# Re-planning the first tile of a fused attention and MLP kernel, and splitting its last store

## Chip, cores and metric

The kernel runs on one core of a Trainium2 chip. The metric is the device time of one execution in microseconds (us). A profile of one execution of the kernel before is at hand: its span (first to last instruction) and the start and length of every instruction on the engines PE (TensorE; PEld is its weight load), DVE (VectorE), ACT (ScalarE), POOL (GpSimd) and SP (the engine that issues most DMAs). Times below are microseconds from the span's start.

## The reference

Attention over 4 batches, 8 heads, 768 positions and head size 64, followed by a two-layer MLP. Some heads ("retrieval") use the full causal mask; the others keep only a few first positions ("sinks") and a window.

```python
scores = scale * np.matmul(q, k.transpose(0, 1, 3, 2))
causal = rel >= 0                      # rel = query position - key position
stream_keep = causal & (is_sink | ((rel >= 0) & (rel < window)))   # 4 sinks, window 64
mask = np.where(retr, causal, stream_keep)                          # per head
a = softmax(np.where(mask, scores, -1e9))
x = matmul(a, v)  ->  [3072 tokens, 512]
h = x @ w_in                           # [3072, 2048]
out = (h - np.tanh(h)) @ w_out         # [3072, 512]
```

## The kernel before

The 3072 tokens are cut into 12 tiles of 256; three tiles make one batch. A tile t is worked in four head pairs; n = 4t + pair numbers the pairs. The stages of a pair:

- `load` (L236): q, k and v of the tile come in as fp32 through SP's queue; the first two tiles in halves of four heads.
- `cast_qk`, `cast_v` (L410 to L449): copies to fp16. v gets a 65th column of ones (scaled), so that the row sum comes out of the same matmul. `scale_v` (L451) makes `vf`, v times a flag per head, for key blocks that lie wholly outside the window: flag 1 for retrieval heads, 0 for the others; there are four such blocks a batch.
- `st_T` (L478): TensorE transposes q and k of the pair into one PSUM tile `tp`; copies take q to `qT` and the two heads of k to `kz`, a buffer of [128, 2, 768] in which each head's rows stand beside zeros. `zero_kz` (L346) writes these zeros once, for two batches' buffers (kz0, kz1).
- `st_S` (L530): scores into a PSUM tile `sc`, exponential on ScalarE into `pt`, and on VectorE a multiplication by the 0/1 mask `m4` (L379), which is built from the select tiles `A4`, `sinks` and the retrieval flags (`retr_i`, `nz`, `rflag`, `thr`).
- `st_A` (L586): `av` = pt times v (and vf); then `rinv` and `x` on VectorE divide by the row sum.
- `st_X` (L628): x is transposed into `xT`, the input of the MLP.

The MLP has `H_unit` (L653: eight matmuls of 256 columns into PSUM `ph`, tanh `th` on ScalarE, `gt` = h - tanh(h) on VectorE; eight units a tile) and `O_mms` (L690: per block of 128 tokens, 16 matmuls of 512 columns into `po`, an eviction on ScalarE to `ot`, a store by SP).

[...] two tiles `sc` of two banks each (used by scores and by tp), one `m` (av, later xp), two `h` (ph), one `o` (po, and xp of the first tile).

The order of the work is not written out by hand. Every stage calls `op` with an engine, a cost in ns, and the keys it reads and writes; the class `Plan` plays the list through with these costs, engine by engine, and at each step emits the ready operation that was recorded first. This settles each engine's instruction order at build time. The semaphores are put in afterwards by the tile framework, from the tiles that instructions touch; they don't depend on the planner's keys. [...]

```python
        for k in r:
            if k in self.writer:
                deps.add(self.writer[k])
            self.readers.setdefault(k, []).append(i)
```

The first tile is recorded pair by pair with its transposes, scores, products; the H units of tile 0 and the attention of tile 1 are laid side by side by a table (`plan`, L784), and the output matmuls of a tile follow one tile later (`LAG`).

Of the kernel before, what the change touches and what calls it, by code (L numbers as in the profile page):

```python
# [7 lines left out]
FP32 = mybir.dt.float32  # L8
FP16 = mybir.dt.float16
I32 = mybir.dt.int32  # L10

XS = 4096.0
TT = 256
NB = TT // 128


class Plan:
# [3 lines left out]

    ENGINES = ("PE", "ACT", "DVE", "POOL", "SP")
    OVERLAP = {"PE": 0, "ACT": 100, "DVE": 88, "POOL": 60, "SP": 0}
    RESULT = {"PE": 200, "ACT": 0, "DVE": 0, "POOL": 0, "SP": 0}

    def __init__(self, bufs):
# [6 lines left out]
    def op(self, eng, ns, fn, r=(), w=(), dma=None, prio=None, port=False):  # L33
        i = len(self.ops)
        deps = set()
        for k in r:
            if k in self.writer:
                deps.add(self.writer[k])
            self.readers.setdefault(k, []).append(i)
        for k in w:  # L40
            if k in self.writer:
                deps.add(self.writer[k])
            deps.update(self.readers.get(k, ()))
            self.writer[k] = i
# [102 lines left out]
def kernel(  # L147
# [12 lines left out]
    nc = tc.nc  # L160
# [115 lines left out]
    def load_w_out(j, w_after):  # L276
# [11 lines left out]

    retr_i = const.tile([128, 2 * H], I32, name="retr_i")
    op(  # L290
        "ACT", 400,
        lambda: nc.scalar.dma_start(
            out=retr_i[:], in_=is_retrieval.bitcast(I32).partition_broadcast(128)
        ),
        w=["retr"], dma=(128, 20.0),
# [50 lines left out]
    def zero_kz(eng, s, hp, c0, c1):  # L346
        op(
            eng, (c1 - c0) * 1.06 + 20,
            lambda: engs[eng].memset(kz[s][hp][:].bitcast(FP32)[:, :, c0 // 2 : c1 // 2], 0.0),  # L349
            w=[("kz", s, hp, g) for g in range(c0 // TT, c1 // TT)],  # L350
        )

    for hp in range(HP):
        zero_kz("DVE", 0, hp, 0, S)

    nz = const.tile([128, 2 * H], FP32, name="nz")
    op(
# [93 lines left out]
    def scale_v(t):  # L451
        b, g = divmod(t, NG)
        v1, vf, lo = v1s[b], vfs[b], g * NB
        for jb in range(lo, min(lo + NB, 4)):
            fl = rflag0 if jb == 0 else rflag
            op(
                "POOL", 1053,
                lambda jb=jb, fl=fl: nc.gpsimd.tensor_mul(  # L458
                    out=vf()[:, jb, :, :], in0=v1()[:, jb, :, :],
                    in1=fl[:].unsqueeze(2).to_broadcast([128, H, D + 1]),  # L460
                ),
                r=[("v1", b, g, 0), ("v1", b, g, 1), "rflag0", "rflag"], w=[("vf", b, jb)],
            )


# [5 lines left out]
    def copy(e, dst, src):  # L471
        if e == "ACT":
            nc.scalar.copy(out=dst, in_=src)  # L473
        else:
            nc.vector.tensor_copy(out=dst, in_=src)  # L475

    def st_T(n, eq="DVE", ek=("DVE", "DVE")):
        t, hp = divmod(n, HP)  # L478
        b, g = divmod(t, NG)
        cs = slice(g * TT, (g + 1) * TT)  # L480
        tp, key = bank([128, 2, NB, 128], FP16, "sc", f"tp{n}")
        cq, ck = t16s["q", t], t16s["k", t]

        def mm():
            for x, c in enumerate((cq, ck)):
                for i in range(NB):
                    nc.tensor.transpose(  # L487
                        out=tp()[:, x, i, :], in_=c()[:, i, 2 * hp : 2 * hp + 2, :],
                        identity=ident16[:],
                    )  # L490

        op(
            "PE", 224, mm,
            r=["ident"] + [("t16" + nm, t, hp * 2 // HP) for nm in "qk"], w=[key],
        )
# [4 lines left out]
        op(  # L500
            eq, cost[eq],
            lambda: copy(eq, qT[n]()[:], tp()[:, 0, :, :].rearrange("p i c -> p (i c)")),
            r=[key], w=[(f"qT{hp}", t)],
        )
        for hh in range(2):
            p_ = slice(64 * hh, 64 * hh + 64)
            op(
                ek[hh], cost[ek[hh]],
                lambda p_=p_, hh=hh: copy(
                    ek[hh], kk[p_, hh, cs], tp()[p_, 1, :, :].rearrange("p i c -> p (i c)")  # L510
                ),
                r=[key], w=[("kz", b % 2, hp, g)],
            )


# [137 lines left out]
    def H_unit(t, u):  # L653
# [33 lines left out]
            r=[key, tk], w=[("gt", t, u)],  # L687
        )

    def O_mms(t, j0, j1):  # L690
        for j in range(j0, j1, 2):
            ts, fb = divmod(j, NFB)
            if fb == 0:
                pos[t] = bank([128, DM], FP32, "o", f"po{t}_{ts}")
            po, key = pos[t]

            def mm(fb=fb, ts=ts, po=po):
                for f in (fb, fb + 1):
                    nc.tensor.matmul(  # L699
                        out=po()[:], lhsT=gts[t]()[:, f, ts * 128 : ts * 128 + 128],  # L700
                        rhs=w_out_t[f // 4]()[:, f % 4, :],
                        start=(f == 0), stop=(f == NFB - 1),
                    )

            op("PE", 2 * 216, mm, r=[("wout", fb // 4), ("gt", t, fb // FU)], w=[key])
            if fb == NFB - 2:
                ot = lazy(o_pool, [128, DM], FP32, "ot", f"ot{t}_{ts}")
                ok = ("ot", 2 * t + ts)
                t0 = t * TT + ts * 128
                op(  # L710
                    "ACT", 597,
                    lambda ot=ot, po=po: nc.scalar.activation(  # L712
                        out=ot()[:], in_=po()[:], func=AF.Copy, scale=1.0 / XS
                    ),
                    r=[key], w=[ok],
                )
                op(
                    "SP", 420,
                    lambda ot=ot, t0=t0: nc.sync.dma_start(out=out[t0 : t0 + 128, :], in_=ot()[:]),
                    r=[ok], dma=(128, 75.0),  # L720
                )


    NU = NTT * HP
# [1 line left out]
    def scores(n):  # L726
        return [lambda gi=gi: st_S(n, gi) for gi in range(len(GROUPS[(n // HP) % NG]))]
# [17 lines left out]
            res.append(lambda: st_X(n))  # L745
        return res

    cast_qk(0, (("DVE", "DVE"), ("ACT", "DVE")), (0,))
    cast_v(0, ("POOL", "POOL"), (0,))
    cast_qk(0, (("DVE", "DVE"), ("DVE", "DVE")), (1,))  # L750
    cast_v(0, ("POOL", "POOL"), (1,))
    load(1, halves=range(2))
    for n in range(HP):
        st_T(n, "ACT", ("DVE", "ACT"))
        if n:
            for f in scores(n - 1):
                f()
        if n > 1:
            st_A(n - 2, 0)
            st_A(n - 2, 1)  # L760
        if n > 2:
            st_X(n - 3, "o")
    for f in scores(HP - 1):
        f()
    for n in (HP - 2, HP - 1):
        st_A(n, 0)
        st_A(n, 1)
        st_X(n - 1, "o")
    st_X(HP - 1, "o")
# [12 lines left out]

# [74 lines left out]
```

The softmax here doesn't subtract the row's maximum and nothing guards it: scores larger than these inputs give would overflow.

## Time and profile before

| what | us |
|---|---|
| median of three runs | 273.51 |
| lowest and highest of them | 271.87, 339.37 |
| the profiled execution | 272.34 |
| its span | 270.5 |
| PE busy in the span | 249.0 (92%) |
| DVE busy | 174.7 (65%) |
| ACT busy | 156.9 (58%) |
| POOL busy | 71.3 (26%) |

In a line of stages the columns are the window, its length, then busy time with the number of instructions for PE, PEld, DVE, ACT and POOL, the granted TensorE clock, the DMA share and GB/s. A line of the chain has start, length and what it was: engine, tile, source line. A line of the timeline has start, length (of all the merged instructions), engine, source line, operation, the tile written and the tile read, the sizes, the count, and in brackets the idle time before it and what ended that. A busy PE is not a PE at its peak, since matmuls overlap and their ends are modelled. Over the whole span the DMA engines are over 90% busy up to about 88 us, while all of q, k, v and the weights come in.

### The profile page before, as it was taken

The page shows a single profiled execution, that of the slowest core. Times are in us where ns is not written, and L with a number is a line of the kernel's source. Part 1 is how long each engine was busy: PE and PEld are TensorE (multiplying, and loading weights), DVE is VectorE, ACT ScalarE, POOL GpSimd, SP SyncE. Part 2 cuts the span into 40 slices and gives each one's busy share as a digit, 9 for nine tenths or more (in the row PEclk, how much of TensorE's full clock was granted, in tenths as well). Part 3 has the DMA queues.
Part 4 walks back from the last instruction along what each step waited for, and adds up shares of the span by engine and source line. Part 5 has one row for each costly group of instructions (what it writes and reads, how often), then busy time and mean ns, then how long its engine had stood idle before and what let it go on. Part 6 is the DMA issues. An engine that isn't in the chain of part 4 may idle for free.

```text
span 270.5 us, 6313 instructions
## 1 busy us (share of the span) xinstructions
PE 249.0 (92%) x2560; PEld 187.1 (69%) x2560; DVE 174.7 (65%) x445; ACT 156.9 (58%) x228; POOL 71.3 (26%) x130
## 2 busy tenths in 40 slices
PE   0477889999999999999999999999999999999974
PEld 0355767777778877777777777777878777776631
DVE  7587765676898765567987746567887555554410
ACT  2355645875567677564577566654657766634420
POOL 7589201364640930309603000300300000000000
PEclk9999999999999999999999999999999999999999
DMA  6999999999998982175631511010001001010101
GB/s 140 221 216 201 196 197 198 226 230 215 245 229 174 199 177 63 43 156 131 139 81 55 106 40 39 2 41 39 15 26 41 2 39 41 2 41 39 41 39 78
DMA packets 82925, 29.78 MB, mean 110 GB/s; under 512 B 75728, under 2 KB 79824, under 8 KB 82896
## 3 DMA queue, kind: packets, MB, share of 16 engines
q1 hardware_dynamic: 78528, 25.17, 43.3%
q0 software_dynamic: 4224, 4.19, 9.2%
q8 instruction: 20, 0.33, 0.5%
q14 instruction: 9, 0.07, 0.1%
q10 hardware_dynamic: 144, 0.01, 0.0%
HBM read 27.27 MB, written 6.29 MB: 124 GB/s over the span
## 4 chain that ended last, share of the span: by engine, by line
PE 86%; DVE 7%; ACT 4%; issue 2%; DVEq 0%
PE po L699 30%; PE ph L663 29%; PE sc L545 14%; PE av L601 8%; PE tp L487 4%; ACT pt L560 2%; PE xp L636 2%; DVE gt L683 1%; DVE pt L572 1%; DVE kz L349 1%; DVE m L383 1%; ACT th L676 1%; DVE x L620 1%; ACT ot L712 1%; DVE nz L359 0%
## 5 line engine op out<-in xcount | busy, mean ns | idle before, releaser
L560 ACT ACTIVATE pt<-sc 128x1024 f16<-128x1024 f32 (+1 forms) x96 | 85.4, 915 | 28.3 <-PE sc L545 25.6
L663 PE MATMUL ph<-xT,win 128*128 128x256 f16 x768 | 100.7, 273 | 0.9 <-DVE gt L683 0.9
L699 PE MATMUL po<-wout,gt 128*128 128x512 f16 x384 | 100.3, 379 | 1.4 <-ACT ot L712 1.4
L676 ACT ACTIVATE th<-ph 128x512 f32<-128x512 f32 x96 | 57.4, 598 | 60.8 <-PE ph L663 57.2
L683 DVE SCALAR_TENSOR_TENSOR gt<-th,ph 128x512 f16<-128x512 f32 x96 | 65.8, 685 | 36.1 <-ACT th L676 35.4
L663 PEld LDWEIGHTS <-win 128*128 128x128 f16 x768 | 71.9, 98 | 14.1 <-issue 1.2
L545 PE MATMUL sc<-qT,kz 128*128 128x128 f16 (+1 forms) x448 | 54.1, 255 | 1.5 <-ACT kz L473 1.3
L699 PEld LDWEIGHTS <-gt 128*128 128x128 f16 x384 | 34.4, 98 | 23.2 <-issue 1.9
L545 PEld LDWEIGHTS <-kz 128*128 128x128 f16 x448 | 38.6, 101 | 13.8 <-issue 1.5
L601 PEld LDWEIGHTS <-pt 128*128 128x128 f16 x672 | 30.1, 99 | 8.0 <-DVE pt L572 2.2
L408 POOL CAST t_q<-raw_q 128x512 f16<-128x512 f32 x22 | 13.5, 625 | 82.6 <-issue 41.1
L601 PE MATMUL av<-v,pt 128*128 128x65 f16 x352 | 29.1, 197 | 1.1 <-DVE pt L572 1.0
L577 DVE TENSOR_TENSOR pt<-pt,m 128x1024 f16<-128x1024 f16 x32 | 22.9, 714 | 8.2 <-ACT pt L560 8.2
L475 DVE COPY kz<-tp 64x256 f16<-64x256 f16 x92 | 26.0, 283 | 2.2 <-ACT qT L473 1.1
L601 PE MATMUL av<-vf,pt 128*128 128x65 f16 x320 | 23.6, 194 | 1.1 <-DVE xT L475 1.1
L487 PE MATMUL tp<-ident,t_q 128*128 128x128 f16 x96 | 13.9, 229 | 10.0 <-DVE t_q L408 9.1
L712 ACT ACTIVATE ot<-po 128x512 f32<-128x512 f32 x24 | 14.3, 598 | 12.7 <-PE po L699 12.5
L615 DVE RECIPROCAL rinv<-av 128x4 f32<-128x4 f32 x48 | 8.6, 180 | 19.4 <-PE av L601 19.4
L620 DVE TENSOR_TENSOR x<-av,rinv 128x256 f16<-128x256 f32 x48 | 20.3, 423 | 1.3
L408 POOL CAST v<-raw_v 128x512 f16<-128x512 f32 x24 | 14.8, 637 | 20.3 <-DMA raw_v<-in_v_dram 20.3
L458 POOL TENSOR_TENSOR vf<-v,rflag 128x520 f16<-128x520 f16 x16 | 18.4, 1170 | 0.4
L487 PEld LDWEIGHTS <-t_q 128*128 128x128 f16 x96 | 8.8, 102 | 13.8 <-DVE t_q L408 9.1
(36 smaller groups left out, 123.1 us busy)
## 6 DMA issues: line engine op xcount, KB each, us to landing
out_dram<-ot SPq DMA_DIRECT2D x24, 256.0 KB, 2.2
raw_q<-in_q_dram SPq DMA_DIRECT2D x20, 256.0 KB, 4.3
raw_k<-in_k_dram SPq DMA_DIRECT2D x20, 256.0 KB, 4.7
raw_v<-in_v_dram SPq DMA_DIRECT2D x20, 256.0 KB, 4.8
win<-in_moe_w_in_dram POOLq DMA_DIRECT2D x4, 512.0 KB, 11.0
wout<-in_moe_w_out_dram POOLq DMA_DIRECT2D x4, 512.0 KB, 19.4
raw_q<-in_q_dram SPq DMA_DIRECT2D x8, 128.0 KB, 3.7
raw_k<-in_k_dram SPq DMA_DIRECT2D x8, 128.0 KB, 3.8
```

The costliest lines, as they stand in the source:

```text
L408: op(e, cost, lambda: engs[e].tensor_copy(out=dst(), in_=src()), r=r, w=w, port=True)
L475: nc.vector.tensor_copy(out=dst, in_=src)
L487: nc.tensor.transpose(out=tp()[:, x, i, :], in_=c()[:, i, 2 * hp : 2 * hp + 2, :], identity=ident16[:],)
L545: nc.tensor.matmul(out=sc()[:, hh, o : o + nb * 128], lhsT=kk[:, hh, jb * 128 : jb * 128 + 128], rhs=qT[n]()[:, q0 * 128 : (q0 + nb) * 128 ...
L560: lambda: nc.scalar.activation(out=pt()[:, :, 512 * gi : 512 * gi + wid], in_=sc()[:, :, 0:wid], func=AF.Exp, scale=inv_sqrt_d,),
L577: nc.vector.tensor_mul(out=pv, in0=pv, in1=m4[:, hs, 256:512].unsqueeze(2).to_broadcast([128, 2, 2, 256]),)
L601: nc.tensor.matmul(out=av()[:, i, hh, :], lhsT=pt()[:, hh, co : co + 128], rhs=vv()[:, jb, h, :], start=(jb == 0), stop=(jb == qb),)
L620: lambda: nc.vector.tensor_mul(out=x16()[:], in0=av()[:, :, :, 0:D], in1=rinv()[:].unsqueeze(3).to_broadcast([128, NB, 2, D]),),
L663: nc.tensor.matmul(out=ph()[:, j, :], lhsT=w_in_t[fb // 4]()[:, cb, f0 : f0 + 128], rhs=xTs[t]()[:, cb, :], start=(cb == 0), stop=(cb == H ...
L676: lambda: nc.scalar.activation(out=th()[:], in_=ph()[:], func=AF.Tanh, scale=1.0 / XS),
L683: lambda: nc.vector.scalar_tensor_tensor(out=gts[t]()[:, u * FU : (u + 1) * FU, :], in0=th()[:], scalar=-XS, in1=ph()[:], op0=ALU.mult, op ...
L699: nc.tensor.matmul(out=po()[:], lhsT=gts[t]()[:, f, ts * 128 : ts * 128 + 128], rhs=w_out_t[f // 4]()[:, f % 4, :], start=(f == 0), stop=( ...
```

## The change

1. The planner gets a rule: two engines that read the same key are ordered if the key's first element is one of `sc`, `m`, `h`, `o`.
2. The retrieval flags are fetched by SP, ahead of q, k and v, and no more by ScalarE.
3. VectorE zeroes only the first 256 columns of kz0; the rest is recorded later, on GpSimd.
4. `scale_v` goes from GpSimd to VectorE.
5. `tp` is laid out over two banks, q in one and k in the other, with a planner key for each.
6. The first tile's casts: q on ScalarE, k on VectorE; the order of its pairs is recorded differently; its kz copies are all on VectorE, its xT copies on ScalarE. The q and k casts of tile 1 go to ScalarE. The w_in loads follow the v casts of tile 1, the w_out loads the last w_in load.
7. In the last tile, block 0 of the output uses the bank `m`; block 1 is computed in two halves of 256 columns, one in `o` (evicted by ScalarE, stored by ScalarE's queue), one in `h` (evicted by VectorE, stored by SP).

```diff
+    PSUM = ("sc", "m", "h", "o")
...
+            if k[0] in self.PSUM:
+                deps.update(j for j in self.readers.get(k, ()) if self.ops[j][0] != eng)
...
-        "ACT", 400,
-        lambda: nc.scalar.dma_start(
+        "SP", 400,
+        lambda: nc.sync.dma_start(
             out=retr_i[:], in_=is_retrieval.bitcast(I32).partition_broadcast(128)
...
     for hp in range(HP):
-        zero_kz("DVE", 0, hp, 0, S)
+        zero_kz("DVE", 0, hp, 0, TT)
...
-                "POOL", 1053,
-                lambda jb=jb, fl=fl: nc.gpsimd.tensor_mul(
+                "DVE", 400,
+                lambda jb=jb, fl=fl: nc.vector.tensor_mul(
...
-        tp, key = bank([128, 2, NB, 128], FP16, "sc", f"tp{n}")
+        tp, key = bank([128, 2, 8, 128], FP16, "sc", f"tp{n}")
+        keys = [(*key, x) for x in range(2)]
...
+    def store(t, ts, po, key, c0, c1, eng, ring):
+        ot = lazy(o_pool, [128, DM], FP32, "ot", f"ot{t}_{ts}_{c0}")
+        rot["ot"] = rot.get("ot", -1) + 1
+        ok = ("ot", rot["ot"])
...
+        op(eng, 110 + 0.95 * (c1 - c0), evac, r=[key], w=[ok])
+        op(
+            ring, 420,
+            lambda: engs[ring].dma_start(out=out[t0 : t0 + 128, c0:c1], in_=ot()[:, c0:c1]),
+            r=[ok], dma=(128, (c1 - c0) * 0.146),
+        )
+
+    def O_group(t, ts, f0, f1, tag, c0=0, c1=DM, eng="ACT", ring="SP"):
+        if f0 == 0:
+            pos[t] = bank([128, DM], FP32, tag, f"po{t}_{ts}_{c0}")
+        po, key = pos[t]
+        def mm():
+            for f in range(f0, f1):
+                nc.tensor.matmul(
+                    out=po()[:, c0:c1], lhsT=gts[t]()[:, f, ts * 128 : ts * 128 + 128],
+                    rhs=w_out_t[f // 4]()[:, f % 4, c0:c1],
+                    start=(f == 0), stop=(f == NFB - 1),
+                )
...
+            if t == NTT - 1 and ts == NB - 1:
+                if fb == 0:
+                    for f in range(0, NFB, 2):
+                        O_group(t, ts, f, f + 2, "o", 0, DM // 2, "ACT", "ACT")
+                    for f in range(0, NFB, 2):
+                        O_group(t, ts, f, f + 2, "h", DM // 2, DM, "DVE", "SP")
+                continue
+            O_group(t, ts, fb, fb + 2, "m" if t == NTT - 1 else "o")
...
-    cast_qk(0, (("DVE", "DVE"), ("ACT", "DVE")), (0,))
...
+    cast_qk(0, (("ACT", "ACT"), ("DVE", "DVE")), (0,))
+    load(1, halves=range(2))
+    for n in (0, 1):
+        st_T(n, "ACT", ("DVE", "DVE"))
+        for f in scores(n):
+            f()
     cast_v(0, ("POOL", "POOL"), (0,))
+    cast_qk(0, (("ACT", "ACT"), ("DVE", "DVE")), (1,))
+    for n in (0, 1):
+        st_A(n, 0)
+        st_A(n, 1)
+        st_T(n + 2, "ACT", ("DVE", "DVE"))
+        for f in scores(n + 2):
+            f()
+        st_X(n, "o", "ACT")
+    cast_v(0, ("POOL", "POOL"), (1,))
+    for n in (2, 3):
+        st_A(n, 0)
+        st_A(n, 1)
+        st_X(n, "o", "ACT")
+    for hp in range(HP):
+        zero_kz("POOL", 0, hp, TT, S)
     for half in range(2):
-        cast_qk(1, (("POOL", "POOL"), ("ACT", "POOL")), (half,))
+        cast_qk(1, (("ACT", "ACT"), ("ACT", "ACT")), (half,))
         cast_v(1, ("POOL", "POOL"), (half,))
     for j in range(4):
-        load_w_in(j, [("t16k", 1, 1)])
+        load_w_in(j, [("v1", 0, 1, j // 2)])
...
     for j in range(4):
-        load_w_out(j, [("v1", 0, 1, 1)])
+        load_w_out(j, [("win", 3)])
     for hp in range(HP):
         zero_kz("POOL", 1, hp, 0, S)
```

More of the change, by code (lines that the diff above doesn't have):

```diff
@@ L461, in scale_v @@
                 ),
-                r=[("v1", b, g, 0), ("v1", b, g, 1), "rflag0", "rflag"], w=[("vf", b, jb)],
+                r=[("v1", b, g, 0), ("v1", b, g, 1), "rflag0", "rflag"], w=[("vf", b, jb)], port=True,
             )
@@ L493, in st_T @@
             "PE", 224, mm,
-            r=["ident"] + [("t16" + nm, t, hp * 2 // HP) for nm in "qk"], w=[key],
+            r=["ident"] + [("t16" + nm, t, hp * 2 // HP) for nm in "qk"], w=keys,
         )
@@ L501, in st_T @@
             eq, cost[eq],
-            lambda: copy(eq, qT[n]()[:], tp()[:, 0, :, :].rearrange("p i c -> p (i c)")),
-            r=[key], w=[(f"qT{hp}", t)],
+            lambda: copy(eq, qT[n]()[:], tp()[:, 0, 0:NB, :].rearrange("p i c -> p (i c)")),
+            r=keys[:1], w=[(f"qT{hp}", t)],
         )
@@ L509, in st_T @@
                 lambda p_=p_, hh=hh: copy(
-                    ek[hh], kk[p_, hh, cs], tp()[p_, 1, :, :].rearrange("p i c -> p (i c)")
+                    ek[hh], kk[p_, hh, cs], tp()[p_, 1, 0:NB, :].rearrange("p i c -> p (i c)")
                 ),
-                r=[key], w=[("kz", b % 2, hp, g)],
+                r=keys[1:], w=[("kz", b % 2, hp, g)],
             )
@@ L688, in H_unit, with evac @@
         )
+    def store(t, ts, po, key, c0, c1, eng, ring):
+        ot = lazy(o_pool, [128, DM], FP32, "ot", f"ot{t}_{ts}_{c0}")
+        rot["ot"] = rot.get("ot", -1) + 1
+        ok = ("ot", rot["ot"])
+        t0 = t * TT + ts * 128
+        def evac():
+            if eng == "ACT":
+                nc.scalar.activation(
+                    out=ot()[:, c0:c1], in_=po()[:, c0:c1], func=AF.Copy, scale=1.0 / XS
+                )
+            else:
+                nc.vector.tensor_scalar(
+                    out=ot()[:, c0:c1], in0=po()[:, c0:c1], scalar1=1.0 / XS, scalar2=None,
+                    op0=ALU.mult,
+                )
[4 more added lines that the diff above has]
+            r=[ok], dma=(128, (c1 - c0) * 0.146),
+        )
+    def O_group(t, ts, f0, f1, tag, c0=0, c1=DM, eng="ACT", ring="SP"):
[8 more added lines that the diff above has]
+                    start=(f == 0), stop=(f == NFB - 1),
+                )
+        op(
+            "PE", (f1 - f0) * 0.422 * (c1 - c0), mm,
+            r=[("wout", f0 // 4), ("gt", t, f0 // FU)], w=[key],
+        )
+        if f1 == NFB:
+            store(t, ts, po, key, c0, c1, eng, ring)
     def O_mms(t, j0, j1):
@@ L692, in O_mms @@
             ts, fb = divmod(j, NFB)
[L693 to L721, printed above, removed]
+            if t == NTT - 1 and ts == NB - 1:
[6 more added lines that the diff above has]
+            O_group(t, ts, fb, fb + 2, "m" if t == NTT - 1 else "o")
     NU = NTT * HP
@@ L746, in slot @@
         return res
-    cast_qk(0, (("DVE", "DVE"), ("ACT", "DVE")), (0,))
-    cast_v(0, ("POOL", "POOL"), (0,))
[L750 to L765, printed above, removed]
+    cast_qk(0, (("ACT", "ACT"), ("DVE", "DVE")), (0,))
[4 more added lines that the diff above has]
+            f()
+    cast_v(0, ("POOL", "POOL"), (0,))
+    cast_qk(0, (("ACT", "ACT"), ("DVE", "DVE")), (1,))
+    for n in (0, 1):
         st_A(n, 0)
         st_A(n, 1)
-        st_X(n - 1, "o")
-    st_X(HP - 1, "o")
+        st_T(n + 2, "ACT", ("DVE", "DVE"))
[9 more added lines that the diff above has]
+        zero_kz("POOL", 0, hp, TT, S)
     for half in range(2):
-        cast_qk(1, (("POOL", "POOL"), ("ACT", "POOL")), (half,))
+        cast_qk(1, (("ACT", "ACT"), ("ACT", "ACT")), (half,))
         cast_v(1, ("POOL", "POOL"), (half,))
     for j in range(4):
-        load_w_in(j, [("t16k", 1, 1)])
+        load_w_in(j, [("v1", 0, 1, j // 2)])
     load(2)
```

## Prediction

> **What bounds the kernel now.** I read the stages first (busy time by window), then the chain that ended last, then the timeline where the chain isn't TensorE.
>
> ```profile
> 0.00:10.00 10.00, 0.88 (x8) 0.77 (x8) 7.58 (x19) 2.35 (x4) 5.96 (x28) 1.00 0.85 167
> 10.00:20.00 10.00, 7.23 (x58) 4.96 (x56) 6.67 (x20) 6.38 (x13) 7.81 (x11) 1.00 1.33 218
> 20.00:30.00 10.00, 7.22 (x80) 5.50 (x80) 7.08 (x21) 4.89 (x6) 7.57 (x10) 1.00 1.22 199
> 120.00:240.00 120.00, 120.00 (x1282) 91.51 (x1280) 82.24 (x214) 75.31 (x108) 17.58 (x32) 1.00 0.18 50
> ```
>
> After the length come PE, PEld, DVE, ACT and POOL. From 50 us on PE is full, so no other engine's saving there is worth anything. The change can only pay where PE has holes: in the first 40 us and at the very end. The chain in the head:
>
> ```profile
> 4.36 1.11 DVE nz L359
> ...
> 6.51 2.22 DVE m L383 x6
> 8.73 0.34 DVE t_q L408
> 9.12 0.62 PE tp L487 x4
> 9.76 0.38 ACT qT L473
> 10.37 0.28 DVE kz L475
> ```
>
> PE starts at 9.12 because VectorE casts q behind its eight m4 rows, which wait for nz. The timeline shows why nz, 16 elements, took 1.18 us:
>
> ```profile
> 3.34 2.09 POOL L349 MEMSET kz<- 128x768 f32 x3
> 4.28 1.18 DVE L359 TENSOR_SCALAR nz<-retr_i 128x16 f32<-128x16 int32 x1
> 5.98 2.75 DVE L383 TENSOR_SCALAR m<-A,thr 128x512 f16<-128x512 f16 x8
> 7.46 0.66 POOL L408 CAST v<-raw_v 128x512 f16<-128x512 f32 x1 [2.03 <-DMA raw_v<-in_v_dram]
> 8.65 0.41 DVE L408 CAST t_q<-raw_q 128x512 f16<-128x512 f32 x1
> ```
>
> nz ends (5.46) when GpSimd's memset run ends (5.43), across a boundary between two memsets: a back-to-back GpSimd run keeps VectorE out. The one m4 of 700 ns (the others 345) lies beside the v cast at 7.46. The tail:
>
> ```profile
> 258.81 3.61 PE L699 MATMUL po<-wout,gt 128*128 128x512 f16 x16 [0.69 <-ACT ot L712]
> 262.46 0.60 ACT L712 ACTIVATE ot<-po 128x512 f32<-128x512 f32 x1 [3.70 <-PE po L699]
> 263.11 3.61 PE L699 MATMUL po<-wout,gt 128*128 128x512 f16 x16 [0.69 <-ACT ot L712]
> 266.76 0.60 ACT L712 ACTIVATE ot<-po 128x512 f32<-128x512 f32 x1 [3.70 <-PE po L699]
> ```
>
> PE waits twice for ScalarE to empty the single "o" bank.
>
> [...] VectorE waited 1.11 us for ScalarE's qT copy before it copied kz from the same tile. [...] a 128x256 sc matmul averages 409 ns from 9 to 24 us and 272 from 26 to 40; four sc matmuls (768 columns) took 0.81 us at 11.48, ten (1792 columns) 0.77 at 45.61; the turn came near 24.7, after PE had been full since 20.80.
>
> **The change, part by part**, in us of the profiled execution (span 270.5, time 272.34, so 1.84 outside it; the median of the runs, 273.51, lies 1.17 above, the lowest 0.47 below).
>
> *To the first transposes.* VectorE zeroes 256 columns of kz instead of 768: four at about 0.28 for 0.81, so it is free at 2.2 and not at 4.28. The flags land 3.1 after issue, as before (issued at 0.81, landed 3.9); leading SP's queue, they push every load back by one issue, 0.42 to 0.5. The rest of kz goes to GpSimd: four memsets of 512, 0.49 each by size from 0.735. In the planner's new order three of them stand ahead of ident, A4 and sinks. The cause is in the diff: the new rule tests k[0], and the string key "ones" begins with "o", so the selects are planned behind ScalarE's warm-up. GpSimd: ones and v memsets to 1.1, three memsets to 2.44, four selects 0.245 apart to 3.42, the fourth memset to 3.86. VectorE: nz at 3.9, rflag, thr, A40 max done at 4.5; GpSimd's last two selects (0.54) to 5.05. m4 could start there, 0.9 earlier than 5.98. But GpSimd has two v memsets (0.17) and the first two kz1 memsets (1.42) queued with no wait between; before, all four ran by 5.43. By the nz pattern m4 waits to 6.55. At 0.263 a row (six between 5.98 and 7.56) five are done when half a tile of v lands (7.42 before, plus 0.45: 7.87). Then GpSimd runs that cast (0.66), two more kz1 memsets (1.42) and a v memset, to 10.0. Three m4 rows to 10.7, then the k cast (0.41): **11.1, against 9.06**. q is cast earlier by ScalarE, which doesn't help: the transposes of k follow those of q. If GpSimd held nothing back it would be 5.05 + 8 x 0.263 + 0.41 = 7.6. I take 11.1; both ends go into the range.
>
> *Pairs of tile 0.* The two banks of tp do not part the readers: in the changed program VectorE's kz copies of pairs 0 and 2 still wait for ScalarE's qT, and ScalarE's qT of pairs 1 and 3 waits for both kz copies (and stands behind ScalarE's other work). So the chain of a pair is qT 0.37 and two kz (0.5), in a row. PE's order is now tp0, sc0, tp1, sc1, av0, tp2 instead of tp0, tp1, sc0, sc1, tp2. With rows of before: k transposes to 11.5, qT 11.9, kz 12.45, sc0 to 13.1, tp1 13.6, kz 14.1, qT 14.5, sc1 to 15.4, av0 15.9. The second half of k is cast behind rinv0, which waits for av0: 16.5, so tp2 ends at 16.9 (13.6 before). x 17.5, sc2 about 18.9, tp3 19.4, two vf products and x on VectorE to 19.9, kz 20.4, qT 20.8: sc3 starts at 20.9 (17.46 before). ScalarE's casts of tile 1 (four at 0.62) stand between exps; av3 and sc4 wait for mask3 behind qT4: sc4 starts at 24.4, not 21.32.
>
> *To the next tile.* Up to the first ph of tile 1 (40.88) both programs hold the same PE work from sc4 on; the new one puts the H units of tile 0 earlier between the scores. Followed the same way (exp 1.03 and 0.81, gt 0.69, ph 0.87 per unit, mask 0.69; half clock until about 30): first ph at 29.7, ph of tile 1 at 43.5. That is **+2.6**. The output matmuls of tile 0 then move behind ph1_2: at sc8 I get 47.1 against 45.61, with six po matmuls (1.3) still owed, +2.8. I carry +2.7. The weights are no issue: win is issued at about 15.9 (17.62 before), and before, ph stood directly behind tp7.
>
> *Far V.* 16 products leave GpSimd (1.17 each). On VectorE the trace has no 520-element fp16 by fp32 product; the nearest, x (256 elements), takes 0.423. [...] Four are in the steps above; the other 12 add 8.4 to a VectorE that is busy 175 of 270, hidden under full PE. From 70 to 80 us it is busy 8.88 of 10, and gt may slip there: 0 to +1.5[...]. I take **+0.2**.
>
> *Tail.* Block 0 of the last tile goes to "m", half a block to "h": both waits of 0.69 (0.65 of it past the eviction) go, -1.35. Halves cost PE nothing: 32 matmuls at 0.109 (ph: 0.87 for eight) for 16 at 0.216. The last eviction is 256 wide on VectorE, 0.3 to 0.35 for 0.60; the last store is half as long, under -0.1. **-1.7**; no one waits for ScalarE's own store, issued earlier.
>
> Sum: 272.34 + 2.7 + 0.2 - 1.7 = **273.5**, +0.4%. What a measurement of this kernel can tell from no change is about 2%, 5.4 us; so the forecast is "within 2%".
>
> **The rivals.**
> *GpSimd gives way* (0.15): single m4 rows slip in, or v lands after they are done, and the k cast ends at 7.6 to 9.1. Then the chain starts 2 to 3.5 earlier, but from about 13 the halves of k and tile 1's loads (0.45 late) hold some of it: head -0.8, so 272.34 - 0.8 + 0.2 - 1.7 = 270.0. For it: the small v memsets at 8.06 let an m4 through. Against it: nz was held across a memset boundary.
> *The array stays at half clock* (0.20): slower by over 2%. [...] PE has 12.8 of full-rate work between sc4 and ph of tile 1; at half rate 12.8 more, of which the 6.3 of waits there hide about half: +6.5 gives 280. It decides once more than 4.3 us of that work runs at half rate beyond mine, that is if the turn comes after about 36. [...]
> *Head absorbed* (0.07): the earlier H units fill all holes, head 0: 270.8.
>
> **How the numbers follow.** The forecast (0.58) spans 271.5 to 276, by 6.55 or 5.05 for m4 and by the vf bound. Faster by over 2% needs -5.4, of which the tail gives 1.7; the 7.6 case passed on whole gives 3.4 more, so 0.05. Slower: the clock case and a bit of the forecast's own edge, 0.22. Range 269.0 to 279.0.
>
> **What would show it.** Right: GpSimd's kz1 memsets beside m4, m4 stretched to over 4 us, first k transposes near 11, sc4 near 24, ph of tile 1 near 43.5; the last three evictions with no PE wait. Wrong: k transposes before 9.5, or PE idle below 7 us after them and before 40.

## The result, and the profile after

The changed kernel takes 275.81 us against 272.93: a ratio of 1.012, interval 1.008 to 1.016. It is slower, by less than 2% but clearly so. One of the four executions of the kernel before took 339.37 us; it pulls up that median and is left out of the ratio. The profiled execution took 276.15 us with a span of 274.4, against 272.34 and 270.5, so 3.9 us more of span. First the same stages as in the prediction, and the one from 70 us:

```profile
0.00:10.00 10.00, 0.40 (x2) 0.13 (x2) 7.21 (x17) 2.10 (x3) 7.41 (x26) 1.00 0.83 170
10.00:20.00 10.00, 5.45 (x42) 3.68 (x43) 6.77 (x20) 4.96 (x9) 5.19 (x13) 1.00 1.33 216
20.00:30.00 10.00, 8.39 (x82) 6.42 (x81) 6.19 (x19) 7.41 (x13) 2.04 (x4) 1.00 1.22 197
70.00:80.00 10.00, 9.05 (x93) 6.31 (x91) 9.64 (x26) 4.71 (x7) 4.76 (x6) 1.00 1.06 205
120.00:240.00 120.00, 118.54 (x1259) 90.39 (x1256) 84.97 (x220) 74.10 (x107) 13.37 (x28) 1.00 0.22 55
```

PE does less by 20 us than it did before (5.9 us busy against 8.1), as forecast. What was not forecast stands in the last two lines: PE has holes from 70 to 80 us and again behind 120, where the kernel before had it busy 9.90 of 10 and 120.00 of 120. From 70 to 80 VectorE is busy 9.64 of 10.

To place a loss, I lined the two traces up by work: the columns of TensorE's matmuls are summed in order, and the time at which each trace reaches the same sum is compared. Both hold the same matmul work (the split block has more and narrower matmuls, but the same columns), so the difference is by how much a kernel is behind.

| stretch (time in the kernel after) | behind the kernel before | forecast |
|---|---|---|
| at 50 to 65 us, after the head | +2.15 | +2.7 |
| from 65 to 139 us | +3.9 more, to +6.06 | +0.2 |
| from 139 us to the last matmuls | 0 | 0 |
| the last 15 us | -2.15 | -1.7 |
| span | +3.9 | +1.2 |

The head and the tail are near the forecast. The loss is in the middle. Its places can be read in the chain of waits; of its longest pieces, these from 60 to 133 us are not on PE (start and length in us, engine and tile):

```profile
64.24 1.22 DVE vf L461 x2
68.50 0.91 DVE pt L576
73.24 2.04 DVE vf L461 x2
93.56 1.02 DVE vf L461
...
128.38 1.13 DVE vf L461
130.42 1.83 DVE vf L461 x3
132.25 0.88 DVE pt L576
```

Five of the seven are far V's products, 7.2 us long; in the kernel before no piece of far V is on the chain. The timeline around the second and around the last two of the seven:

```profile
73.15 2.13 DVE L461 TENSOR_TENSOR vf<-v,rflag 128x520 f16<-128x520 f16 x2
...
73.66 2.10 POOL L411 CAST t_k<-raw_k 128x512 f16<-128x512 f32 x2
...
75.21 0.27 DVE L478 COPY kz<-tp 64x256 f16<-64x256 f16 x1
...
75.54 0.34 PE L549 MATMUL sc<-qT,kz 128*128 128x256 f16 x2 [0.71 <-DVE kz L478]
```

```profile
130.34 1.91 DVE L461 TENSOR_TENSOR vf<-v,rflag 128x520 f16<-128x520 f16 x3
...
132.17 0.96 DVE L576 TENSOR_TENSOR pt<-pt,m 128x768 f16<-128x768 f16 x1
...
133.72 0.41 DVE L624 TENSOR_TENSOR x<-av,rinv 128x256 f16<-128x256 f32 x1
...
134.18 0.29 PE L640 MATMUL xp<-ident,x 128*128 128x128 f16 x2 [1.46 <-DVE x L624]
```

Two products that take 2.13 us together (GpSimd's casts run beside them, and are longer too: 2.10 for two where one takes 0.61 alone) stand ahead of a kz copy of 0.27 us in VectorE's order, and PE's next matmul waits 0.71 for it. At 130 it is three products, then a mask product and a gt, and PE waits 1.46 for x. PE's longer waits for VectorE's tiles from 60 to 140 us (total us, times, longest):

```profile
PE xp L640 <- DVE x L624: 1.5, 1, 1.5
PE sc L549 <- DVE kz L478: 1.2, 3, 0.7
```

They are 0.71, 0.17, 0.28 and 1.46, together 2.6. The view counts a wait from the modelled end of the matmul before it. The next could have started 0.16 earlier: a matmul of 256 columns is 0.27 long, but one starts every 0.11. From start to start, the four waits delay PE by 0.87, 0.33, 0.44 and 1.62, together 3.3. Two more for x, at 66.5 and 70.5, delay it by 0.5, and delays of 0.15 and less add up to 0.7, where the kernel before has 0.6 in all: that is the 3.9. A single product costs a twelfth of the 8.4 us that the prediction has for twelve:

```profile
L461 DVE TENSOR_TENSOR vf<-v,rflag x16: 690/700/1142, 17.6 to 131.6; 128x520 f16<-128x520 f16 x16
```

The middle one of the three durations (min, median, max in ns) is 0.70. The 8.4 was the author's estimate; gt in the kernel before, 512 elements in 0.685 us, gives the same 0.70 by size.

The start of the head is in kind as foretold:

```profile
3.38 0.65 DVE L362 TENSOR_SCALAR nz<-retr_i 128x16 f32<-128x16 int32 x1 [1.35 <-DMA retr_i<-in_is_retrieval_dram]
...
5.18 1.41 POOL L352 MEMSET kz<- 128x768 f32 x2
5.20 5.23 DVE L386 TENSOR_SCALAR m<-A,thr 128x512 f16<-128x512 f16 x8 [0.43 <-POOL A L316]
...
7.16 0.61 POOL L411 CAST v<-raw_v 128x512 f16<-128x512 f32 x1 [0.56 <-DMA raw_v<-in_v_dram]
7.71 1.41 POOL L352 MEMSET kz<- 128x768 f32 x2
...
10.35 0.41 DVE L411 CAST t_k<-raw_k 128x512 f16<-128x512 f32 x1
```

Eight m4 rows take 5.23 us beside the kz1 memsets and v's cast, and k is cast by 10.76. At the end, PE runs its last 52 po matmuls without a wait, and what follows is short:

```profile
263.15 7.97 PE L726 MATMUL po<-wout,gt 128*128 128x512 f16 x52
...
267.67 0.60 ACT L702 ACTIVATE ot<-po 128x512 f32<-128x512 f32 x1 [2.86 <-PE po L726]
269.42 0.38 ACT L702 ACTIVATE ot<-po 128x256 f32<-128x256 f32 x1 [1.15 <-PE po L726]
...
271.23 0.42 DVE L706 TENSOR_SCALAR ot<-po 128x256 f32<-128x256 f32 x1 [6.55 <-PE po L726]
```

### The profile page after: what moved, and what is told of

Read it like the earlier page. It is cut to its first block, busy times and chain, and to the rows that moved or that the text cites. A ratio compares the mean times of both kernels' runs of the same rounds, so it can differ in the third digit from the quotient of the medians.

```text
span 274.4 us, 6365 instructions
## 1 busy us (share of the span) xinstructions
PE 249.4 (91%) x2576; PEld 187.6 (68%) x2576; DVE 185.7 (68%) x461; ACT 158.6 (58%) x232; POOL 54.6 (20%) x115
## 4 chain that ended last, share of the span: by engine, by line
PE 78%; DVE 15%; ACT 3%; issue 1%; DMA 1%; POOL 0%; ACTq 0%; DVEq 0%
PE po L726 27%; PE ph L667 26%; PE sc L549 13%; PE av L605 7%; DVE vf L461 4%; PE tp L491 3%; DVE gt L687 3%; DVE kz L478 2%; PE xp L640 2%; DVE m L386 2%; ACT pt L564 1%; DVE x L624 1%; DVE pt L576 1%; DMA retr_i<-in_is_retrieval_dram 1%; DVE xT L478 1%
## 5 line engine op out<-in xcount | busy, mean ns | idle before, releaser
L564 ACT ACTIVATE pt<-sc 128x1024 f16<-128x1024 f32 (+1 forms) x96 | 85.5, 916 | 29.9 <-PE sc L549 29.7
L726 PE MATMUL po<-wout,gt 128*128 128x512 f16 (+1 forms) x400 | 100.3, 370 | 0.0
L726 PEld LDWEIGHTS <-gt 128*128 128x128 f16 x400 | 35.8, 98 | 19.6
L549 PEld LDWEIGHTS <-kz 128*128 128x128 f16 x448 | 37.5, 100 | 16.5 <-DVE kz L478 4.1
L411 POOL CAST t_q<-raw_q 128x512 f16<-128x512 f32 x20 | 12.6, 638 | 95.0 <-issue 80.8
L478 DVE COPY kz<-tp 64x256 f16<-64x256 f16 x96 | 27.3, 284 | 3.3 <-PE tp L491 1.0
L411 POOL CAST v<-raw_v 128x512 f16<-128x512 f32 x24 | 16.5, 717 | 24.5 <-DMA raw_v<-in_v_dram 24.5
L702 ACT ACTIVATE ot<-po 128x512 f32<-128x512 f32 (+1 forms) x24 | 14.2, 590 | 10.6 <-PE po L726 10.5
L491 PE MATMUL tp<-ident,t_k 128*128 128x128 f16 x96 | 14.0, 230 | 5.5 <-DVE t_k L411 5.5
L640 PE MATMUL xp<-ident,x 128*128 128x128 f16 x96 | 13.7, 226 | 3.4 <-DVE x L624 3.2
```

The costliest lines, as they stand in the source:

```text
L411: op(e, cost, lambda: engs[e].tensor_copy(out=dst(), in_=src()), r=r, w=w, port=True)
L491: nc.tensor.transpose(out=tp()[:, x, i, :], in_=c()[:, i, 2 * hp : 2 * hp + 2, :], identity=ident16[:],)
L549: nc.tensor.matmul(out=sc()[:, hh, o : o + nb * 128], lhsT=kk[:, hh, jb * 128 : jb * 128 + 128], rhs=qT[n]()[:, q0 * 128 : (q0 + nb) * 128 ...
L564: lambda: nc.scalar.activation(out=pt()[:, :, 512 * gi : 512 * gi + wid], in_=sc()[:, :, 0:wid], func=AF.Exp, scale=inv_sqrt_d,),
L726: nc.tensor.matmul(out=po()[:, c0:c1], lhsT=gts[t]()[:, f, ts * 128 : ts * 128 + 128], rhs=w_out_t[f // 4]()[:, f % 4, c0:c1], start=(f == ...
```

## The experiments

Each ratio is to the kernel before, run beside it on the same chip.

### One part undone, one part alone

**Far V back on GpSimd** (e1), in the changed kernel. The planner is still told of a VectorE operation, so the order of TensorE, ScalarE and VectorE otherwise stays.

```diff
-                lambda jb=jb, fl=fl: nc.vector.tensor_mul(
+                lambda jb=jb, fl=fl: nc.gpsimd.tensor_mul(
```

> The changed kernel with the 16 far-V products issued on GpSimd again; the planner still plans them as VectorE work, so that all other engines keep the changed kernel's order. Theory A (the products on VectorE stall TensorE after the head: by matched matmul work the changed kernel loses 3.9 us between 65 and 140 us): those losses go, the time falls by 3 to 4.5 us, to 271.3 to 272.8, and the steps at about 67, 74, 95 and 133 us are gone from the curve of matched work. Theory B (the new order itself makes those stalls, whoever does the products): the time stays within 1 us of the changed kernel, 275 or more.

Measured: 270.52 us, ratio 0.993 (0.990 to 0.995). Lined up by work, it is 0.3 us ahead of the kernel before at 48 us and at the last matmuls: no loss is left in the middle, and PE is full again:

```profile
120.00:240.00 120.00, 120.00 (x1285) 91.65 (x1284) 82.09 (x214) 75.08 (x108) 17.20 (x32) 1.00 0.18 50
```

So far V on VectorE costs 5.3 us by the medians and 6.3 by the profiled spans. Of the 6.3, 3.9 lie in the middle and 2.4 in the head, where two products stand ahead of kz copies between 17 and 20 us and two ahead of gt between 30 and 32; all four are on the chain of waits there, with 2.8 us. The profiled execution of e1 is one of its fastest (269.88), so by the medians the head's share is nearer 1.4. The gain is larger than expected, since the share in the head was not thought of. In this kernel k is still cast as late as 10.37 us, and yet the head is not behind.

**The kz1 memsets later** (e2): the changed kernel, with the four memsets of 768 columns issued behind the last load of w_out.

```diff
     def load_w_out(j, w_after):
...
-            lambda: nc.gpsimd.dma_start(
+            lambda: (nc.gpsimd.dma_start(
...
-            ),
+            ), [f() for f in held if j == 3]),
...
     def zero_kz(eng, s, hp, c0, c1):
+        def clear():
+            engs[eng].memset(kz[s][hp][:].bitcast(FP32)[:, :, c0 // 2 : c1 // 2], 0.0)
...
-            lambda: engs[eng].memset(kz[s][hp][:].bitcast(FP32)[:, :, c0 // 2 : c1 // 2], 0.0),
+            (lambda: held.append(clear)) if s == 1 else clear,
```

> The changed kernel with its four kz1 memsets moved on GpSimd from beside the m4 rows to behind the last w_out load; all other orders kept. Theory C (those memsets hold VectorE back and set the start of the chain): the eight m4 rows take about 2.2 us instead of 5.2, the k cast ends near 8 instead of 10.8, the scores of tile 1 start 1.5 to 3 us earlier than at 23.9, and the end comes 1 to 2.5 earlier. Theory D (the head is set by the new order of the pairs, by later loads and by ScalarE's queue): m4 gets shorter, but the scores of tile 1 start less than 0.7 earlier and the end moves by less than 0.7.

Measured: 273.53 us, ratio 1.003 (1.001 to 1.005).

```profile
5.20 2.19 DVE L391 TENSOR_SCALAR m<-A,thr 128x512 f16<-128x512 f16 x8 [0.43 <-POOL A L316]
...
7.30 0.42 DVE L416 CAST t_k<-raw_k 128x512 f16<-128x512 f32 x1
```

The rows take 2.19 us where they took 5.23, from the same start. The scores of tile 1 start at 21.1 instead of 23.9. After the head the kernel is 0.2 us ahead of the one before instead of 2.15 behind; the waits of 0.71, 0.28 and 1.46 us in the middle are all still there. The time falls by 2.3 us, so it is shown that the memsets beside m4 cause a loss in the head.

**Far V on VectorE alone** (e3), put into the kernel before:

```diff
-                lambda jb=jb, fl=fl: nc.gpsimd.tensor_mul(
+                lambda jb=jb, fl=fl: nc.vector.tensor_mul(
```

> The kernel before with only the far-V products moved to VectorE, in the places where GpSimd had them; the planner still plans them as GpSimd work, so nothing else moves. Theory A: slower by 2 to 5 us, about 275 to 278, with TensorE waits where the products stand in front of kz, x or gt. Theory B: within 1 us of the kernel before.

Measured: 275.24 us, ratio 1.011 (1.008 to 1.013). PE's waits from 60 to 140 us, in the same columns as above (the kernel before has none over 0.25 us):

```profile
PE sc L545 <- DVE kz L475: 1.7, 3, 0.8
```

The same mechanism in another order: three copies of kz come late, each behind a single product, two of them with a gt or an xT copy between. The loss needs neither the rest of the change nor products in a row.

**The new tail alone** (e4), put into the kernel before: `store`, `O_group` and `O_mms` of the change.

> The kernel before with only the last tile's output changed (banks m, o and h, the last block in two halves). The prediction's tail step gives -1.7 us; the two traces give -2.1 by the time from the last tile's first output matmul to the end of the span. Expected 270.8 to 271.3 against 272.9. A rival (the second queue or the narrow store gives it back): no gain over 0.5.

Measured: 270.04 us, ratio 0.994 (0.991 to 0.996). It is 2.05 us below the kernel before, which took 272.09 beside it: more than the prediction's 1.7, and near the 2.15 of the table.

### Do the two losses of the head add up?

**Both undone** (e5): the edits of e1 and e2 together.

> The changed kernel with both undone parts at once: far V's products back on GpSimd, and the four kz1 memsets behind the last w_out load. Each alone brought the stretch from 50 us on to 0.2 to 0.3 us ahead of the kernel before; far V alone also removed the 3.9 us of stalls between 69 and 139 us. Theory O (the two head losses hide one another: what binds the head then is the rest, the loads and the chain of a pair): the combination is worth what far V on GpSimd alone is worth, 270.0 to 270.8 us. Theory S (they add, since they stand at different places, 7.8 to 11 us and 17 to 32 us): the head gains another 2.0 to 2.4 us, 268.0 to 268.7. The step to look at is the time of the first ph matmul of tile 0 and of sc of tile 1, against the two single edits.

Measured: 269.81 us, ratio 0.992 (0.989 to 0.995); the executions spread from 268.0 to 271.9, the profiled one took 268.42. In its trace the head is 2.2 us ahead of the kernel before, where e1 and e2 were 0.3 and 0.2 ahead. So in that execution they add nearly in full, 4.35 of 4.85. The median says otherwise. It lies just below the range of theory O, over 1 us above that of theory S, and only 0.3 us (by the ratios, whose intervals overlap) to 0.7 us (by the medians) below e1. Whether the two losses add in a typical execution stays open. The spread is taken up at the end.

### Load or placement?

**The true cost for the planner** (e6): far V stays on VectorE in the changed kernel.

```diff
-                "DVE", 400,
+                "DVE", 700,
```

> The changed kernel with far V on VectorE still, but its cost told to the planner as 700 ns and not 400; the planner then writes another order on every engine. Theory P (it is the placement: the planner believes VectorE has room it hasn't, and puts two or three products back to back ahead of kz and x): with the true cost the stalls of 0.71, 0.28 and 1.46 us between 69 and 139 us go, and the time falls to 270.5 to 272. Theory L (it is the load: VectorE is busy 9.6 of 10 us there whatever the order, so the delay is only moved): 274.5 to 276.5.

Measured: 272.52 us, ratio 1.001 (1.000 to 1.002), between the two theories. Products of 0.69 us as before, a wholly different order. The head is 0.15 behind instead of 2.15, and the middle loses 1.85 us instead of 3.9. So with the same products on the same engine 3.3 us, by the medians, hung on a wrong number in the planner, through the order it wrote. The new order differs everywhere, in the head too, so what was won behind far V is not separated from what was won elsewhere. What is left in the middle is many small waits (the only one above 0.25 is 0.55 at 65 us, for an eviction by ScalarE).

**fp16 flags** (e7), in the changed kernel and its order:

```diff
-    rflag = const.tile([128, H], FP32, name="rflag")
+    rflag = const.tile([128, H], FP16, name="rflag")
```

(and `rflag0` alike.)

> The changed kernel in the same order, with far V on VectorE, but its two flag tiles are fp16 and not fp32 (the flags are 0 or 1). Only the length of the 16 products can change. If the product of two fp16 tensors takes the same 0.69 us as with the fp32 flag, nothing moves: 275.3 to 276.3. If it is faster (about 0.35, as the mask product of 768 fp16 elements at 0.56 suggests by size: 0.38), the 16 products give back 5.4 us of VectorE time, the back-to-back groups of two and three last 0.8 to 1.1 us instead of 1.9 to 2.1, and the stalls at 74.8, 95.7 and 132.7 go or shrink: 271 to 273.5. That would say the duration of the product, and not the engine it is on, is the price.

Measured: 276.01 us, ratio 1.013 (1.011 to 1.016), and the product takes 700 ns as ever. The type of the flag is not what sets its length. My 0.38 was sized from a product whose two inputs are dense; here the flag is read as a broadcast, 65 times each.

**Dense fp16 flags** (e13) tests whether the broadcast is what sets it: the flags are written out once to [128, 520].

```diff
+                lambda i=i, fl=fl: nc.vector.tensor_copy(
+                    out=dense[i][:], in_=fl[:].unsqueeze(2).to_broadcast([128, H, D + 1])
+                ),
...
-            fl = rflag0 if jb == 0 else rflag
+            fl = dense[0 if jb == 0 else 1]
...
-                    in1=fl[:].unsqueeze(2).to_broadcast([128, H, D + 1]),
+                    in1=fl[:],
```

> The changed kernel with far V on VectorE at the planner's cost of 400, but with the flags written out once as dense fp16 tiles of 128x520 (two extra copies of about 0.6 us each behind the second half of tile 0's v). e7 changed only the flag's type and left its product at 0.69 to 0.70; there the flag was still read as a broadcast. Theory D (the product is slow because its flag is a broadcast and not dense): the dense product scales from the mask product of 768 dense fp16 elements at 0.56 and of 1024 at 0.69, 0.52 ns an element, to 0.43 for 520; the planner's 400 is then nearly true, the stalls of 0.71, 0.28 and 1.46 us shrink or go, and 3 us of the 3.9 between 50 and 139 us come back: 272 to 274. Theory N (0.69 is the price of any 520-element product): 275.5 to 277.

Measured: 271.30 us, ratio 0.996 (0.994 to 0.998), better than expected.

```profile
L473 DVE TENSOR_TENSOR vf<-v,dense x16: 408/428/852, 19.2 to 127.9; 128x520 f16<-128x520 f16 x16
```

0.43 us a product for 0.70: with dense flags it is shorter, and the planner's 400 is nearly true. The head is 0.1 behind the kernel before and the middle loses 1.6: of the 3.9, 2.3 come back and not 3, and the rest of the gain is in the head. Of the waits, 0.63 remains at 72 us, and those of 0.28 and 1.46 are gone. The two extra copies move the order of all engines, so length and order are not separated here, but against the changed kernel some 4.4 us come back with far V still on VectorE.

### The claims on the head

**The selects planned first** (e10), in the changed kernel:

```diff
-            if k[0] in self.PSUM:
+            if isinstance(k, tuple) and k[0] in self.PSUM:
```

> The changed kernel with one thing more: the planner's new rule asks whether a key is a tuple, so that the string 'ones' is no longer taken for an 'o' bank. GpSimd's order becomes ones, v memsets, four selects, then the kz memsets, as before the change; TensorE's order stays. The prediction named this mix-up as the reason why the selects are late. Theory A (the selects' place is the cause of the late m4): m4 starts before 4.7 and its eight rows end near 7 to 8, k cast near 8.5, first ph of tile 0 near 26: 273 to 274.5. Theory B (the memset run is the cause, wherever the selects stand; nz or m4 is held by whichever memsets are running): nz or m4 is held to about 6 and the k cast ends at 9.8 to 10.8, so the time is that of the changed kernel within 0.7: 275.1 to 276.3.

Measured: 275.96 us, ratio 1.014 (1.012 to 1.016): nothing, as theory B has it.

```profile
3.04 1.45 POOL L352 MEMSET kz<- 128x512 f32 x3
...
3.37 2.57 DVE L362 TENSOR_SCALAR nz<-retr_i 128x16 f32<-128x16 int32 x1 [0.97 <-DMA retr_i<-in_is_retrieval_dram]
...
4.50 1.41 POOL L352 MEMSET kz<- 128x768 f32 x2
...
6.46 3.66 DVE L386 TENSOR_SCALAR m<-A,thr 128x512 f16<-128x512 f16 x8
```

With the selects out of the way nz, 16 elements, is held for 2.57 us, to the end of a run of memsets at 5.91, then the rows take 3.66, and the cast of k starts at 10.04, as against 10.35. The mix-up of "ones" with an "o" bank is real, but it costs nothing measurable: here the memsets hold nz (2.57 us for 0.65), in the changed kernel the m4 rows (5.23 for the 2.19 of e2).

**k of tile 0 in a bank of its own** (e9): e5 with the k transposes of the first four pairs in an "h" tile. The planner writes its order anew.

```diff
+        if n < 4:
+            tk, kkey = bank([128, NB, 128], FP16, "h", f"tk{n}")
+            keys = [key, kkey]
...
-                        out=tp()[:, x, i, :], in_=c()[:, i, 2 * hp : 2 * hp + 2, :],
+                        out=tk()[:, i, :] if x and tk else tp()[:, x, i, :], in_=c()[:, i, 2 * hp : 2 * hp + 2, :],
```

> The kernel of e5 with the k transposes of the four pairs of tile 0 in a tile of their own (one of the h banks), so that the two halves of tp are two tiles and not two banks of one tile. The planner writes its order anew. Theory R (the readers are serialised because they read one tile, as in the trace, where kz waits 0.89 us for ScalarE's qT at 8.6): with two tiles kz starts with the end of the transposes, 0.37 us earlier in each of four pairs; sc0 starts 0.35 us earlier, and the head gains 0.5 to 1.3 us, so 0.5 to 1.3 below e5. Theory N (PE is what binds the head after the kz1 memsets are out of the way, or the loads of k's second half): sc0 starts earlier but the first ph does not, and the time is that of e5 within 0.4.

Measured: 268.00 us, ratio 0.985 (0.981 to 0.989). In the changed kernel kz waits for qT from the same tile; in e9 it starts with the transposes:

```profile
11.24 0.37 ACT L476 COPY qT<-tp 128x256 f16<-128x256 f16 x1 [6.04 <-PE tp L491]
...
11.65 0.61 DVE L478 COPY kz<-tp 64x256 f16<-64x256 f16 x2 [0.89 <-ACT qT L476]
```

```profile
8.22 1.25 DVE L483 COPY kz<-tk 64x256 f16<-64x256 f16 x4 [0.49 <-PE tk L500]
8.44 0.37 ACT L481 COPY qT<-tp 128x256 f16<-128x256 f16 x1 [2.39 <-PE tp L500]
8.56 0.13 PEld L559 LDWEIGHTS <-kz 128*128 128x128 f16 x2 [0.21 <-DVE kz L483]
```

(First the changed kernel, then e9.) The first kz copy starts 0.41 us behind qT in the changed kernel and 0.22 ahead of it in e9. So two banks of one tile do not part the readers, and two tiles do: the order of the readers goes by the tile, not by the bank. In the profiled executions the gain over e5 is 0.8 us of span; in the medians 1.8, with spreads of 3 and 4 us, so its size stays loose.

**e9 with far V on VectorE at the true cost** (e11):

> The kernel of e9 with far V on VectorE again, told to the planner at 700 ns (as in e6). It asks what is left against VectorE when the head is mended and the planner knows the cost. Theory L (load: e6 still lost 1.85 us between 63 and 135 us against the kernel before, without a large single stall): 1.5 to 2.5 us above e9, 269.5 to 270.5. Theory P (placement alone): within 0.7 of e9, 267.5 to 268.7.

Measured: 269.71 us, ratio 0.991 (0.989 to 0.993), 1.7 above e9. By work it loses 1.85 us between 63 and 135 us, as e6 did, and e9 none. With the head mended and the planner told, VectorE is still the dearer engine for this product with its broadcast flag.

**e9 with a truthful planner** (e12): far V planned as what it is there, a GpSimd product of 1053 ns, and the mended rule of e10.

> The kernel of e9 with the planner told the truth on both counts: far V as a GpSimd product of 1053 ns (e9 runs it there but plans it on VectorE at 400), and the mended key rule of e10. In the trace of e9 TensorE is full from 41 us on, so only the first 40 us can move: 266.5 to 268.5 if the order of the head gets better, and 268 to 269.5 if far V's products on GpSimd are now planned ahead of the loads of weights or the kz memsets.

Measured: 267.63 us, ratio 0.982 (0.979 to 0.986), not told apart from e9. Both beat the kernel before, by 4 to 5 us, and the changed one, by 7 to 8.

## Why the prediction was wrong

It forecast 273.5 us, +0.4%, and took that for no difference; the kernel takes 275.81 and is 1.2% slower. All the signs that it named for being right came true, from the stretched m4 to the three evictions without a wait. They lie in the head and the tail; none looks at the stretch between, whose cost it had put near nothing. By its steps:

- **To the first transposes: right in kind.** m4 held at the start by the kz1 memsets, then v's cast, then two more memsets: k cast ends at 10.76, forecast 11.1. Two terms were off. The flags landed 2.5 us after their issue and not 3.1. And v's first half, which was to come 0.45 later than before, is cast at 7.16, where it was 7.46: so three rows were done and not five when the second hold began. That the selects are planned behind the warm-up is true and, by e10, without price. (In the lines of before, not all other rows take 345 ns: the one after the row of 700 takes 547, beside the v memsets at 8.06.)
- **Pairs of tile 0 and the next tile: right.** sc3 at 20.70 (20.9), sc4 at 23.93 (24.4), first ph of tile 0 at 28.53 (29.7), ph of tile 1 at 42.54 (43.5), sc8 at 46.46 (47.1). The head costs 2.15 where 2.7 stood. That the sum fits is in part luck. The forecast put nearly all of it on the late k cast. In the profiled executions the late k cast and the four early far V products each cost over 2 us, and undoing either one brings the head level with before; without both (e5) it is 2.2 ahead. So the rest of the new head gains about as much as one of the two loses, and the working had no such gain. Which part of the change gives it was not taken apart, and by the medians it is smaller.
- **Far V: the step that failed.** "The other 12 add 8.4 to a VectorE that is busy 175 of 270, hidden under full PE", +0.2 with an upper end of +1.5. The price of one, 0.70 by that 8.4, was right. Measured: +3.9 in the middle in this change, +2.8 in the kernel before (e3: from 0.6 us ahead after the head to 2.2 behind), and 5.3 to 6.3 with the head (e1). Three things were left out of the sum. First, an engine with idle time on average is not idle where the product stands (VectorE is busy 9.64 of 10 us from 70 to 80): two or three products in a row put 1.9 to 2.1 us ahead of a kz copy or an x that PE needs within less, and in e3 single products were enough. That PE is full makes a saving on another engine worthless; it does not make added work there free. Secondly, the planner has 0.40 where the chip takes 0.70, and the working priced the 0.70 only as load: told 700, the planner wrote an order in which the kernel, with the same products, takes 3.3 us less (e6). Thirdly, six of the 16 products stand beside GpSimd's casts and last 1.10 to 1.14, with casts of up to 1.08 for 0.61; the working had all at 0.70.
- **Tail: right, and undersized.** Both waits go. The end of the last matmul comes 1.65 us nearer to that of before (1.35 forecast). The last eviction on VectorE takes 0.42 for a forecast of 0.3 to 0.35. From its end to the end of the span it is 2.76 us, where 3.12 were before: the half store gives 0.36, forecast under 0.1.
- **The rivals.** GpSimd did not give way (m4 5.23 us, not 2.2). What the prediction calls half clock is the slower of two rates of TensorE: in e4 a ph matmul starts every 0.21 us at it, in the kernel before every 0.11 at the faster one. The granted clock reads 1.00 at both. In the profiled execution the faster one held from 27 us on (the working had about 30; what brings it was not shown), so the slow rate did not decide. Nor does the turn at 27 instead of 24.7 make the loss in the head: in e10's profiled execution, with the time of the changed kernel, the 256-column sc matmuls near 26 us took 269 to 273 ns, where those of the changed kernel took 370 to 417, and its head was 2.0 behind all the same. The head was not absorbed.

The sum with the measured terms is 272.34 + 2.15 + 3.9 - 2.15 = 276.2, against 276.15. With far V's middle at its measured size, the prediction's own head and tail would have given 277.2, which is slower.

## What to carry to other kernels

Full TensorE hid VectorE's added work here only as long as nothing it needed was queued behind that work; where something was, 3.9 us were lost in the middle, and 2.8 in e3. Before costing an operation at nothing, name what stands behind it on its queue and how soon that is due. When a hand-fed planner decides the order, check the costs it is fed against the trace: 400 for 700 ns was worth 3.3 us here, through the order of everything. And an operation is priced with its operands' form: the same product is 0.70 us with a broadcast flag and 0.43 with a dense one.

## What the runs showed of the hardware

- **Back-to-back GpSimd memsets can hold VectorE over instruction boundaries.** nz takes 0.65 us beside one memset, 1.18 in the kernel before beside a run of three, and 2.57 in e10 beside a longer one; it ends 0.03 us after the run each time. Eight m4 rows take 2.19 us in e2, with GpSimd idle from 5.28 to 7.32, and 5.23 beside four memsets and a cast: two rows bear it all, with 1.54 and 2.20 us. But a run need not hold. In e10 the same cast and the last two memsets take turns with the rows from 7.2 to 9.6 us; no row takes over 0.90, and those memsets take 0.87 and 0.88 for 0.73. Which of the two happens is not explained here. (Durations in ns, min, median and max: the changed kernel, then e10.)

```profile
L386 DVE TENSOR_SCALAR m<-A,thr x8: 332/340/2201, 5.2 to 10.1; 128x512 f16<-128x512 f16 x8
```

```profile
L386 DVE TENSOR_SCALAR m<-A,thr x8: 335/350/900, 6.5 to 9.8; 128x512 f16<-128x512 f16 x8
```

- **Far V's product beside GpSimd casts, in the changed kernel:** 1.10 to 1.14 us for 0.70, and casts up to 1.08 for 0.61. In e6 it fell on GpSimd alone: two products at 71.2 us kept their 0.68, and the cast beside them took 1.90.
- **TensorE's slow rate ends at times that differ from one execution to the next.** In the profiled execution of e4, which has the head of the kernel before, ph matmuls between 28 and 33 us took 421 ns; in the kernel before, 273 (from start to start 0.21 us for 0.11):

```profile
L663 PE MATMUL ph<-xT,win x11: 421/421/421, 30.8 to 32.9; 128*128 128x256 f16 x11
```

```profile
L663 PE MATMUL ph<-xT,win x18: 271/273/273, 29.9 to 33.0; 128*128 128x256 f16 x18
```

By work, that execution fell 2.3 us behind there; it took 272.61, as four others of e4's 19 did within 0.1, while the other 14 took 269.4 to 270.2. The granted clock in the lines of stages reads 1.00 from 28 to 33 us in both, so it does not show this. What sets the time of the change was not shown. It may be what spreads e5, e9 and e12 over 3 us, but only one execution of each was profiled, so that is argued and not shown.
